# One fixed place order for VectorE's side work in a fused attention, expert and cosine kernel

## The chip, the core and the metric

The kernel runs on one core of a Trainium2 chip. The metric is the device time of one execution in microseconds (us). Three runs of the kernel before gave 2160.01, 2161.22 and 2163.99 us; the median is 2161.22.

## The reference

Three layers follow one another. A delta-rule attention gives 3072 tokens of 384 numbers. A mixture of 8 experts follows, in which every token goes through every expert, and each expert's result is scaled by a probability; the probabilities come from an exponential and eight rounds of row and column normalising. A network with `h * cos(h)` ends it.

```
P = np.exp(logits)                       # 3072 x 8
for _ in range(8):
    P /= P.sum(1, keepdims=True) + 1e-09
    P /= P.sum(0, keepdims=True) + 1e-09
    P *= N / E
for e in range(E):
    h = np.maximum(x @ w1[e], 0.0)       # 384 -> 1024
    ye = h @ w2[e]                       # 1024 -> 384
    out += P[:, e:e + 1] * ye
...
h = x @ w_in; g = h * np.cos(h); return g @ w_out
```

## The kernel before

Everything is float32, computed as a high and a low part that are both rounded to the matmul's input format: one product is three matmuls (high by high, high by low, low by high).

Attention and expert 0 come first, to about 412 us of the profile. Then experts 1 to 7 run in 56 **groups** of one function, `group(n)`. A group holds 256 of an expert's 1024 hidden units. The tokens are handled in two passes of 1536: groups 0 to 27 are the first pass, 28 to 55 the second. Inside a group three token blocks by two halves of hidden units are multiplied with a fast scheme that needs 15 products where the plain one needs 18. Its products have names and a fixed order: N0, N2, N1, N4, N3, CE, b, a, CD, DF, EF, CF, d, c, e, each three matmuls of 512 columns (L1456). They go into five accumulator banks that change roles from group to group (X, Z, A, B, C). ScalarE copies some banks out (`copy`, L1461), VectorE adds and subtracts between them (`vadd`, L1464: seven in a group, called here by their results B, A, sc, s2, C, Z and the second B). A product that adds to a bank, or reuses it, waits for these: **CE** needs B done, since B still reads Z; **a** needs A; **EF** needs sc, since sc reads Z; **c** needs C.

Between the products stand six blocks of nine matmuls of the second layer (L150), after N2, N4, CD, CF, c and e. Twelve such blocks, four for each of three token blocks, are spread over an odd group and the even one behind it. After the fourth block of a token block `gates()` multiplies the three result banks by the expert's probabilities (L1488, VectorE, three instructions) and adds them to the running sum (L1489, GpSimd, three). That falls after N3 and after e in odd groups, and after CF in even ones.

Each engine works through its own instructions in the written order. Beside the above, a group carries **side work**:

- `s_prep(n + 1)` makes the next group's first weights: in the first pass GpSimd forms sums (q0, q1: L1257 to L1265), ScalarE rounds the high parts (`hi`, L1268), VectorE subtracts for the low parts (`lo`, L1271); they are also stored, and the second pass only loads them (`g_load`, L1227).
- `w2h`, `w2l` split the second weights in the same way (L1281 on ScalarE; L1285 on VectorE in the first pass, on GpSimd in the second).
- `bgq` is a list of small pieces that `bg()` takes from: first the token sums of the second pass (`t_prog`), then the **weight conversion** of the last network, nine VectorE instructions per half block (L1419 to L1427, called c0 to c8 below), 288 in all.

`s_prep` gives lists that the group runs at seven places, `go(0)` to `go(6)`; `bg()` stands at eight places.

The probabilities reach the chip's memory once (`pts`). `p_load` (L1309) brings one expert's row for 512 tokens into `pslot[t]`, copied to all partitions: 512 runs of 512 bytes, issued by SyncE. Expert 0's result was stored unscaled; `acc_load` brings it back (L1314) and `acc_mul` scales it by expert 0's probabilities on GpSimd (L1324, nine instructions). In group 0 the three slots get expert 0's rows, in group 1 expert 1's rows go into the same three slots.

Of the kernel before, what the change touches and what calls it, by code (L numbers as in the profile page):

```python
# [38 lines left out]
def kernel(  # L39
# [654 lines left out]
    with tc.manual_schedule():  # L694
# [337 lines left out]
        def t_prog(p, s, rest):  # L1032
# [32 lines left out]
            def emit(nm, i, hi, also=None):  # L1065
                gap(3)

                def run():
                    v.tensor_tensor(out=s[i].bitcast(F32R), in0=s[i], in1=s[hi], op=SUB)
                    keep(nm, hi, 0)  # L1070
                    keep(nm, i)
                    if also and not rest:
                        keep(*also)
                    if not rest:
                        put()
                q.append(lambda: nc.scalar.activation(out=s[hi].bitcast(F32R), in_=s[i], func=ACTF.Copy))
# [164 lines left out]
        def w2_get(n):  # L1241
            nc.sync.dma_start(out=w2reg(n)[:, 768:1536].bitcast(F32), in_=w2c[n % GP])

        def s_prep(n):

# [32 lines left out]

            def w2h():
                x = w2reg(n)  # L1280
                nc.scalar.activation(out=x[:, 0:768], in_=x[:, 768:1536].bitcast(F32), func=ACTF.Copy)  # L1281

            def w2l():
                x = w2reg(n)
                (nc.gpsimd if n >= GP else nc.vector).tensor_tensor(  # L1285
                    out=x[:, 768:1536], in0=x[:, 768:1536].bitcast(F32), in1=x[:, 0:768].bitcast(F32), op=ALU.subtract
                )

            def raw_next():
# [4 lines left out]
            if n >= GP:  # L1294
                return [[lambda: g_load(n)], [], [get], [], [], [w2h], [w2l]]
            return [[q0, q1, hi(s_p, ps)], [lo(s_p, ps), hi(s_v, vs)],
                    [get, hi(s_f, fs), lo(s_f, fs), lo(s_v, vs)],
                    [raw_next, hi(s_u, us)], [lo(s_u, us)], [store, w2h], [w2l]]

# [7 lines left out]

        def p_load(t, e, b):
            nc.sync.dma_start(  # L1309
                out=pslot[t].rearrange("p (t c) -> p t c", t=4), in_=pts[4 * b:4 * b + 4, e, :].partition_broadcast(128)  # L1310
            )

        def acc_load(p, t):
            nc.sync.dma_start(out=acc3[t], in_=ysc[3 * p + t])  # L1314

        def acc_mul(p, t):
            b, z = 3 * p + t, ctile(3) if p else pslot[t]
            if p:
                nc.sync.dma_start(
                    out=z.rearrange("p (t c) -> p t c", t=4), in_=pts[4 * b:4 * b + 4, 0, :].partition_broadcast(128)  # L1320
                )
# [29 lines left out]
        def temit(nm):  # L1351
# [7 lines left out]
                [lambda: temit("CE"), lambda: x2sum(2), lambda: tadd("d", 0)],  # L1359
                sq[3] + [lambda: temit("CD"), lambda: tadd("e", 1)], sq[4], sq[5][:1]]  # L1360
        nb = 0
# [145 lines left out]

        def bg(k=1, opt=False):
            if opt and gnow[0] < GP and len(bgq) <= len(cv):
                return  # L1510
            for _ in range(k if gnow[0] > 1 else 0):
                if bgq:
                    bgq.pop(0)()

        def group(n):
# [9 lines left out]
            if n + 4 < GP:  # L1525
                w2_copy(n + 4)
            nx = s_prep(n + 1) if n + 1 < NGR else [[] for _ in range(7)]
            if n == 0:
                nx[0] = [lambda: tadd("CF", 2), cfirst, lambda: tadd("c", 2), lambda: temit("CF")] + nx[0]
                nx[1] = [lambda: temit("d")] + nx[1] + [lambda: w2_get(0)]  # L1530
                nx[2] = [lambda: temit("c")] + nx[2] + [lambda: temit("e")]
                nx[3] = nx[3] + sq[5][1:]
                nx[4] = nx[4] + sq[6]

# [25 lines left out]
            gates()  # L1560
            bg()
            m(X, "N1")
# [3 lines left out]
            vadd(B, sb, Z, ALU.subtract)  # L1566
            bg(opt=True)
            F()
# [6 lines left out]
            gates()  # L1575
            go(1)
            bg(2 if p else 1)
            m(Z, "CE")
# [3 lines left out]
            relu(n, 0, 0, A)  # L1582
            bg()
            m(X, "CD")
# [235 lines left out]
        bg(999)  # L1820

# [86 lines left out]
```

## Time and profile before

| | |
|---|---|
| time of the profiled execution | 2159.15 us |
| span of its trace | 2157.4 us |
| TensorE matmul busy | 2071.0 us, 96% |
| VectorE busy | 1433.3 us, 66% |
| GpSimd busy | 939.2 us, 44% |
| ScalarE busy | 858.3 us, 40% |

TensorE's busy share covers the whole span; where it idles has to be looked up by stage. The groups run from 412.08 to 1738.84 us. In a row of instructions "ps" is an accumulator bank, "mh" a hidden tile, "w1t" and "w2t" weight tiles, "tp" the buffers of the conversion, "cth" and "scr" scratch tiles, "accp" the running sums. The arrow at a row's end names what ended the idle time before it.

### The profile page before, as it was taken

What the parts mean: (1) busy time and instruction counts of PE and PEld (TensorE: products, weight loads), DVE (VectorE), ACT (ScalarE), POOL (GpSimd) and SP (SyncE); (2) the same over time, 40 slices, a digit from 0 to 9 for tenths busy, and PEclk for the clock granted to TensorE, in tenths of its full rate; (3) what the DMA queues carried; (4) which work ended last, traced back from release to release, by engine and by line L of the source; (5) the groups of instructions that cost most, each with busy time, mean ns of one, the idle gap of its engine ahead of it and who ended that gap; (6) DMA issues with size and microseconds to landing.
All of it is one profiled execution on the core that took longest, in us unless ns stands there. A gap on an engine that the chain in (4) does not pass through costs nothing.

```text
span 2157.4 us, 39716 instructions
## 1 busy us (share of the span) xinstructions
PE 2071.0 (96%) x16147; PEld 1729.1 (80%) x16147; DVE 1433.3 (66%) x2231; ACT 858.3 (40%) x1436; POOL 939.2 (44%) x1029
## 2 busy tenths in 40 slices
PE   7899999879999999999999999999999999999999
PEld 6788888657787887777777888878888889999998
DVE  6665445656766776776767777777777656666665
ACT  3333223333343343333323333323233246666665
POOL 4676560546465564444435333333334343333332
PEclk7899999989999999999999999999999999999999
DMA  5433244755455555344494534344353370001000
GB/s 95 120 91 83 47 114 147 273 169 199 173 178 172 168 182 172 137 154 166 173 332 152 184 127 167 131 137 163 115 176 127 140 290 7 23 30 30 15 16 15
DMA packets 210742, 290.72 MB, mean 135 GB/s; under 512 B 85968, under 2 KB 159152, under 8 KB 210560
## 3 DMA queue, kind: packets, MB, share of 16 engines
q1 hardware_dynamic: 207728, 281.41, 39.5%
q0 software_dynamic: 1664, 6.49, 0.9%
q8 instruction: 126, 2.06, 0.4%
q10 hardware_dynamic: 1168, 0.30, 0.1%
q14 instruction: 56, 0.46, 0.1%
HBM read 187.12 MB, written 112.03 MB: 139 GB/s over the span
## 4 chain that ended last, share of the span: by engine, by line
PE 75%; DVE 9%; POOL 6%; issue 3%; DMA 3%; ACT 1%; SPq 1%; POOLq 0%; DVEq 0%; ACTq 0%
PE ps L150 29%; PE ps L1456 19%; PE ps L1735 9%; PE ps L1693 9%; PE ps L138 4%; DVE cth L1488 2%; POOL accp L1489 2%; DVE mh L157 2%; PE ps L312 1%; DMA w2t<-w2c 1%; DVE scr L1464 1%; DVE tp L1420 1%; POOL w1t L391 1%; POOL w1t L387 1%; PE ps L280 1%
## 5 line engine op out<-in xcount | busy, mean ns | idle before, releaser
L150 PE MATMUL ps<-mh,w2t 128*128 128x512 f32 x3060 | 751.9, 390 | 11.4 <-DVE cth L1488 11.4
L150 PEld LDWEIGHTS ps<-mh,w2t 128*128 128x128 f32 x3060 | 576.5, 189 | 132.9 <-DVE cth L1488 12.3
L1456 PE MATMUL ps<-T,w1t 128*128 128x512 f32 x2520 | 640.5, 393 | 35.5 <-DVE scr L1464 27.8
L1489 POOL TENSOR_TENSOR accp<-accp,cth 128x512 f32<-128x512 f32 x246 | 337.5, 1402 | 633.4 <-DVE cth L1488 633.4
L1456 PEld LDWEIGHTS ps<-T,w1t 128*128 128x128 f32 x2520 | 468.4, 188 | 153.9 <-DVE scr L1464 42.7
L156 ACT ACTIVATE mh<-ps 128x512 fp32r<-128x512 f32 x340 | 201.5, 597 | 525.5 <-DVE ps L1464 194.7
L157 DVE SCALAR_TENSOR_TENSOR mh<-ps,mh 128x512 fp32r<-128x512 f32 x340 | 227.7, 686 | 165.2 <-ACT mh L156 165.1
L1464 DVE TENSOR_TENSOR ps<-scr,ps 128x512 f32<-128x512 f32 x168 | 116.7, 694 | 153.8 <-PE ps L1456 152.1
L1461 ACT ACTIVATE scr<-ps 128x512 f32<-128x512 f32 x224 | 134.1, 599 | 210.3 <-PE ps L1456 202.5
L1702 POOL TENSOR_SCALAR tp<-tp 128x512 f32<-128x512 f32 x92 | 91.2, 992 | 204.4 <-ACT tp L1701 204.4
L1488 DVE TENSOR_TENSOR cth<-ps,scr 128x512 f32<-128x512 f32 x246 | 154.2, 683 | 23.9 <-issue 17.1
L1716 DVE TENSOR_TENSOR tp<-tp,ps 128x512 f32<-128x512 f32 x96 | 66.1, 688 | 133.5 <-ACT tp L1715 133.5
L138 PE MATMUL ps<-xb,w1t 128*128 128x512 f32 x432 | 113.1, 406 | 4.9 <-DVE h L157 3.5
L1464 DVE TENSOR_TENSOR scr<-ps,scr 128x512 f32<-128x512 f32 x112 | 76.8, 686 | 38.1 <-PE ps L1456 37.4
L150 PE MATMUL ps<-h,w2t 128*128 128x512 f32 x396 | 98.4, 393 | 0.0
L138 PEld LDWEIGHTS ps<-xb,w1t 128*128 128x128 f32 x432 | 79.0, 191 | 23.3 <-DVE h L157 3.6
L391 POOL TENSOR_TENSOR w1t<-w1t 128x30 f32<-128x30 f32 (+9 forms) x150 | 81.9, 546 | 11.8
L150 PEld LDWEIGHTS ps<-h,w2t 128*128 128x128 f32 x396 | 73.4, 188 | 15.5
L1693 PE MATMUL ps<-xx,cw 128*128 128x512 f32 x360 | 84.0, 390 | 0.0
L387 POOL TENSOR_TENSOR w1t<-Nsys,w1t 128x30 f32<-128x30 f32 (+9 forms) x150 | 77.2, 515 | 11.4
L1701 ACT ACTIVATE tp<-ps 128x512 f32<-128x512 f32 x96 | 56.2, 586 | 63.7 <-PE ps L1693 63.7
L1735 PE MATMUL ps<-cw,nh 128*128 128x384 f32 x432 | 78.6, 335 | 0.0
(281 smaller groups left out, 2762.4 us busy)
## 6 DMA issues: line engine op xcount, KB each, us to landing
wss<-w1t SPq DMA_DIRECT2D x56, 768.0 KB
w1t<-wss SPq DMA_DIRECT2D x56, 768.0 KB
w2t<-w2c SPq DMA_DIRECT2D x56, 384.0 KB
wsn<-tp SPq DMA_DIRECT2D x64, 192.0 KB
scr<-pts SPq DMA_DIRECT2D x45, 256.0 KB
wraw<-in_moe_w_dram SPq DMA_DIRECT2D x28, 384.0 KB
w2c<-in_moe_w_dram SPq DMA_DIRECT2D x28, 384.0 KB
wss<-w1t SPq DMA_DIRECT2D x28, 384.0 KB
```

The costliest lines, as they stand in the source:

```text
L138: nc.tensor.matmul(out=ps[:, :nn], lhsT=w[:, a, kk, fs], rhs=x[:, b, kk, c0:c0 + nn], start=(i == 0), stop=(i == 3 * KD - 1),)
L150: nc.tensor.matmul(out=banks[kd], lhsT=w[:, a, f % 2, kd * 128:(kd + 1) * 128], rhs=h[:, b, :], start=(first and b == 0 and a == 0), stop= ...
L156: nc.scalar.activation(out=h[:, 0, :nn], in_=ps[:, :nn], func=ACTF.Relu)
L157: nc.vector.scalar_tensor_tensor(out=h[:, 1, :nn], in0=ps[:, :nn], scalar=0.0, in1=h[:, 0, :nn].bitcast(F32), op0=ALU.max, op1=ALU.subtract,)
L391: eng.tensor_tensor(out=xsys[:, j + 1:, 0:j], in0=xsys[:, j + 1:, 0:j], in1=a, op=ALU.add)
L1456: nc.tensor.matmul(out=bank, lhsT=s_of(n, nm, a), rhs=T[:, b, :], start=start and q == 0, stop=q == 2, skip_group_check=True)
L1461: nc.scalar.activation(out=out, in_=in_, func=ACTF.Copy, scale=scale)
L1464: nc.vector.tensor_tensor(out=out, in0=a, in1=b, op=op)
L1488: nc.vector.tensor_tensor(out=c, in0=yb[kd], in1=pslot[t], op=ALU.mult)
L1489: nc.gpsimd.tensor_tensor(out=a[:, kd, :], in0=a[:, kd, :], in1=c, op=ALU.add)
L1693: nc.tensor.matmul(out=hb2(i), lhsT=net_w1(f, a, kk), rhs=x2[b](c, kk), start=(j == 0), stop=(j == 3 * KD - 1))
L1735: nc.tensor.matmul(out=ybk[t][:, :DM], lhsT=h[:, a, ts], rhs=net_w2(f, c), start=(f == 0 and j == 0), stop=(f == FT2 - 1 and j == 2),)
```

## The change

Five things are done.

1. The eight places of `bg()` become four: after the block behind N2, after the sum B (behind N4), behind CD, and at the group's end. How many pieces are taken there depends on what the list holds: 2, 2, 2, 2 of the token sums; 1, 0, 2, 1 of the conversion in the first pass; 3 (4 in odd groups), 2, 3, 2 in the second.
2. `go(1)`, which holds the `lo` of the SP weights in the first pass, moves from behind N3 to before N1; the `hi` of the SV weights moves from `go(1)` to `go(2)`.
3. The second weights are split in the group that uses them: `w2h(n)` before N1, `w2l(n)` behind the sum B, where before group n - 1 did it at its end.
4. Expert 0's row for the first token block goes into a scratch tile (`ctile(3)`), so that `pslot[0]` gets expert 1's row at once. For the other two blocks expert 1's row is loaded right behind the scaling, and GpSimd issues that load.
5. A rounding step of the token sums comes one empty piece later (`gap(4)`).

```diff
-        def bg(k=1, opt=False):
-            if opt and gnow[0] < GP and len(bgq) <= len(cv):
-                return
+        def bg(sums, first, second):
+            k = second if gnow[0] >= GP else sums if len(bgq) > len(cv) else first
...
             gates()
-            bg()
+            if n:
+                w2h(n)
+            go(1)
+            bg(2, 1, 3 + n % 2)
             m(X, "N1")
...
             vadd(B, sb, Z, ALU.subtract)
-            bg(opt=True)
+            if n:
+                w2l(n)
+            bg(2, 0, 2)
...
             gates()
-            go(1)
-            bg(2 if p else 1)
             m(Z, "CE")
...
             relu(n, 0, 0, A)
-            bg()
             m(X, "CD")
...
             go(2)
-            bg()
+            bg(2, 2, 3)
...
         def acc_mul(p, t):
-            b, z = 3 * p + t, ctile(3) if p else pslot[t]
+            b, z = 3 * p + t, ctile(3) if p or not t else pslot[t]
...
+            if not p and t:
+                p_load(t, 1, t, nc.gpsimd)
...
             if not sk:
+                z_load(0, ctile(3))
                 for t in range(3):
-                    p_load(t, 0, t)
+                    p_load(t, 0 if t else 1, t)
```

The order of three places follows; "ps_154" are the accumulator banks, and lines from L1242 on are numbered differently in the two kernels (conversion L1419 to L1427 before, L1423 to L1431 after; `vadd` L1464 and L1468; `gates` L1488 and L1492).

VectorE in an odd group of the second pass (35), from the sum A to the sum sc, before:

```order
L1464 TENSOR_TENSOR ps_154<-scr,ps_154 128x512
L1488 TENSOR_TENSOR cth<-ps_154,scr 128x512 x3
L1419 TENSOR_SCALAR tp<-tp 128x384
L1420 TENSOR_SCALAR tp<-tp 128x384
L157 SCALAR_TENSOR_TENSOR mh<-ps_154,mh 128x512 x2
L1421 SCALAR_TENSOR_TENSOR tp<-tp 128x384
L1464 TENSOR_TENSOR scr<-ps_154,scr 128x512
```

The same place after:

```order
L1468 TENSOR_TENSOR ps_154<-scr,ps_154 128x512
L1492 TENSOR_TENSOR cth<-ps_154,scr 128x512 x3
L157 SCALAR_TENSOR_TENSOR mh<-ps_154,mh 128x512 x2
L1468 TENSOR_TENSOR scr<-ps_154,scr 128x512
L1423 TENSOR_SCALAR tp<-tp 128x384
```

Three conversion pieces have left the stretch between the sums A and sc.

VectorE from the end of odd group 35 into even group 36, before, from `gates()` to the sum A:

```order
L1488 TENSOR_TENSOR cth<-ps_154,scr 128x512 x3
L157 SCALAR_TENSOR_TENSOR mh<-ps_154,mh 128x512
L1425 TENSOR_SCALAR tp<-tp 128x384
L1426 SCALAR_TENSOR_TENSOR tp<-tp 128x384
L1464 TENSOR_TENSOR ps_154<-scr,ps_154 128x512
L1427 SCALAR_TENSOR_TENSOR tp<-tp 128x384
L1464 TENSOR_TENSOR ps_154<-scr,ps_154 128x512
```

The same place after:

```order
L1492 TENSOR_TENSOR cth<-ps_154,scr 128x512 x3
L157 SCALAR_TENSOR_TENSOR mh<-ps_154,mh 128x512
L1426 TENSOR_SCALAR tp<-tp 128x384
L1427 SCALAR_TENSOR_TENSOR tp<-tp 128x384
L1428 TENSOR_SCALAR tp<-tp 128x384
L1429 TENSOR_SCALAR tp<-tp 128x384
L1430 SCALAR_TENSOR_TENSOR tp<-tp 128x384
L1468 TENSOR_TENSOR ps_154<-scr,ps_154 128x512
L1431 SCALAR_TENSOR_TENSOR tp<-tp 128x384
L1423 TENSOR_SCALAR tp<-tp 128x384
L1468 TENSOR_TENSOR ps_154<-scr,ps_154 128x512
```

Five pieces instead of two stand ahead of the sum B, and two instead of one between B and A.

SyncE's transfers at the end of group 0 and in group 1, before ("accp<-ysc" is expert 0's result, "w2c" and "wraw" are weights):

```order
L654 DMA pts<-scr 64x128
L1309 DMA scr<-pts 128x4x128 x3
L1314 DMA accp_6359<-ysc_83 128x1536
L1314 DMA accp_6360<-ysc_84 128x1536
L1314 DMA accp_6361<-ysc_85 128x1536
L1236 DMA w2c_102<-in_moe_w_dram 256x1x384
L1242 DMA w2t<-w2c_99 128x768
L1230 DMA wraw<-in_moe_w_dram 128x3x256
L1309 DMA scr<-pts 128x4x128 x3
```

After:

```order
L654 DMA pts<-scr 64x128
L1316 DMA cth<-pts 128x4x128
L1308 DMA scr<-pts 128x4x128 x3
L1313 DMA accp_6359<-ysc_83 128x1536
L1313 DMA accp_6360<-ysc_84 128x1536
L1313 DMA accp_6361<-ysc_85 128x1536
L1236 DMA w2c_102<-in_moe_w_dram 256x1x384
L1242 DMA w2t<-w2c_99 128x768
L1230 DMA wraw<-in_moe_w_dram 128x3x256
```

A fourth row of probabilities stands ahead of the other loads, and the three later ones have left the queue.

## Rows read from the trace of the kernel before

**Rows 1.** The page's head.
```profile
span 2157.4 us, 39716 instructions
```

**Rows 2.** Busy time by stretch: group 2; 3-27; 28-54; 35; 36. Then clock, DMA share, GB/s.
```profile
465.06:501.95 36.89, 25.53 (x101) 20.04 (x100) 15.32 (x24) 9.46 (x17) 27.88 (x26) 0.81 0.68 243
501.95:1087.50 585.55, 570.77 (x2477) 461.57 (x2476) 412.89 (x614) 226.23 (x406) 301.82 (x300) 1.00 0.50 172
1087.50:1716.03 628.53, 610.99 (x2675) 500.55 (x2674) 454.92 (x716) 198.14 (x325) 233.44 (x163) 1.00 0.46 159
1252.18:1276.11 23.93, 22.75 (x100) 18.51 (x99) 14.85 (x26) 7.33 (x12) 4.81 (x4) 1.00 0.25 91
1276.11:1298.55 22.44, 22.44 (x100) 18.59 (x99) 18.55 (x28) 7.32 (x12) 11.24 (x8) 1.00 0.56 164
```

**Rows 3.** TensorE's waits: for whom, us in total, times, longest.
```profile
PE ps L1456 <- DVE scr L1464: 27.8, 28, 1.7
PE ps L150 <- DVE cth L1488: 11.4, 1, 11.4
```

**Rows 4.** Timeline of groups 35, 36: start, us, engine, instruction, count, [idle before].
```profile
1262.26 0.48 DVE L1419 TENSOR_SCALAR tp<-tp 128x384 f32<-128x384 f32 x1
1262.77 1.34 DVE L1420 TENSOR_SCALAR tp<-tp 128x384 int32<-128x384 int32 x1
1265.23 0.55 DVE L1421 SCALAR_TENSOR_TENSOR tp<-tp 128x384 f32<-128x384 f32 x1
1266.44 1.66 PE L1456 MATMUL ps<-T,w1t 128*128 128x512 f32 x6 [1.18 <-DVE scr L1464]
...
1278.33 1.13 DVE L1425 TENSOR_SCALAR tp<-tp 128x384 int32<-128x384 int32 x1
1279.50 1.52 DVE L1426 SCALAR_TENSOR_TENSOR tp<-tp 128x384 int32<-128x384 int32 x1
1281.75 1.39 DVE L1427 SCALAR_TENSOR_TENSOR tp<-tp 128x384 fp32r<-128x384 int32 x1
1282.91 3.56 PE L1456 MATMUL ps<-T,w1t 128*128 128x512 f32 x15
1284.40 0.36 DVE L1419 TENSOR_SCALAR tp<-tp 128x384 f32<-128x384 f32 x1
```

**Rows 5.** GpSimd beside them, in group 36.
```profile
1276.70 3.91 POOL L1489 TENSOR_TENSOR accp<-accp,cth 128x512 f32<-128x512 f32 x3 [11.43 <-DVE cth L1488]
1280.57 2.15 POOL L1285 TENSOR_TENSOR w2t<-w2t 128x768 fp32r<-128x768 f32 x1
```

**Rows 6.** Timeline of first-pass groups 20 (ScalarE) and 21.
```profile
908.70 0.63 ACT L1268 ACTIVATE w1t<-scr 128x512 fp32r<-128x512 f32 x1 [5.53 <-POOL scr L1265]
...
932.00 0.81 DVE L1271 TENSOR_TENSOR w1t<-wraw,w1t 128x512 fp32r<-128x512 f32 x1
932.74 1.64 DVE L1426 SCALAR_TENSOR_TENSOR tp<-tp 128x384 int32<-128x384 int32 x1
936.70 1.65 PE L1456 MATMUL ps<-T,w1t 128*128 128x512 f32 x6 [1.70 <-DVE scr L1464]
```

**Rows 7.** Timeline around group 2's wait, all engines.
```profile
474.31 0.84 ACT L1281 ACTIVATE w2t<-w2t 128x768 fp32r<-128x768 f32 x1 [11.12 <-DMA w2t<-w2c]
475.54 0.62 ACT L1268 ACTIVATE w1t<-wraw 128x512 fp32r<-128x512 f32 x1
468.79 11.07 POOL L1324 TENSOR_TENSOR accp<-accp,scr 128x512 f32<-128x512 f32 x9 [18.42 <-DMA accp<-ysc]
488.69 0.45 POOL L1265 TENSOR_TENSOR scr<-wraw 128x128 f32<-128x128 f32 x1
477.94 4.21 PE L150 MATMUL ps<-mh,w2t 128*128 128x512 f32 x9 [11.36 <-DVE cth L1488]
481.94 2.01 PE L1456 MATMUL ps<-T,w1t 128*128 128x512 f32 x6
```

**Rows 8.** A stretch of 4 us there, in the columns of rows 2.
```profile
460.00:464.00 4.00, 4.00 (x20) 3.30 (x19) 1.82 (x4) 1.45 (x3) 0.00 (x0) 1.00 0.78 68
```

More of the change, by code (lines that the diff above doesn't have):

```diff
@@ L1065, in emit @@
             def emit(nm, i, hi, also=None):
-                gap(3)
+                gap(4)
                 def run():
@@ L1242, in w2_get, with w2h, w2l @@
             nc.sync.dma_start(out=w2reg(n)[:, 768:1536].bitcast(F32), in_=w2c[n % GP])
+        def w2h(n):
+            x = w2reg(n)
+            nc.scalar.activation(out=x[:, 0:768], in_=x[:, 768:1536].bitcast(F32), func=ACTF.Copy)
+        def w2l(n):
+            x = w2reg(n)
+            (nc.gpsimd if n >= GP else nc.vector).tensor_tensor(
+                out=x[:, 768:1536], in0=x[:, 768:1536].bitcast(F32), in1=x[:, 0:768].bitcast(F32), op=ALU.subtract
+            )
         def s_prep(n):
@@ L1277, in store @@
                     nc.sync.dma_start(out=wss[n % GP][:, o:o + t.shape[1]], in_=t.bitcast(F32))
[L1279 to L1287, printed above, removed]
             def raw_next():
@@ L1294, in s_prep @@
             if n >= GP:
[L1295 to L1298, printed above, removed]
+                return [[lambda: g_load(n)], [], [get], [], [], []]
+            return [[q0, q1, hi(s_p, ps)], [lo(s_p, ps)], [get, hi(s_v, vs), hi(s_f, fs), lo(s_f, fs), lo(s_v, vs)],
+                    [raw_next, hi(s_u, us)], [lo(s_u, us)], [store]]
         def t_load(p, nm):
@@ L1306, in t_load, with p_load @@
             nc.sync.dma_start(out=TT[nm].bitcast(F32), in_=src)
-        def p_load(t, e, b):
-            nc.sync.dma_start(
+        def p_load(t, e, b, eng=nc.sync):
+            eng.dma_start(
                 out=pslot[t].rearrange("p (t c) -> p t c", t=4), in_=pts[4 * b:4 * b + 4, e, :].partition_broadcast(128)
@@ L1314, in acc_load, with z_load @@
             nc.sync.dma_start(out=acc3[t], in_=ysc[3 * p + t])
+        def z_load(b, z):
+            nc.sync.dma_start(
+                out=z.rearrange("p (t c) -> p t c", t=4), in_=pts[4 * b:4 * b + 4, 0, :].partition_broadcast(128)
+            )
         def acc_mul(p, t):
-            b, z = 3 * p + t, ctile(3) if p else pslot[t]
+            b, z = 3 * p + t, ctile(3) if p or not t else pslot[t]
             if p:
-                nc.sync.dma_start(
-                    out=z.rearrange("p (t c) -> p t c", t=4), in_=pts[4 * b:4 * b + 4, 0, :].partition_broadcast(128)
-                )
+                z_load(b, z)
             for kd in range(KD):
@@ L1359 @@
                 [lambda: temit("CE"), lambda: x2sum(2), lambda: tadd("d", 0)],
-                sq[3] + [lambda: temit("CD"), lambda: tadd("e", 1)], sq[4], sq[5][:1]]
+                sq[3] + [lambda: temit("CD"), lambda: tadd("e", 1)], sq[4], sq[5]]
         nb = 0
@@ L1526, in group @@
                 w2_copy(n + 4)
-            nx = s_prep(n + 1) if n + 1 < NGR else [[] for _ in range(7)]
+            nx = s_prep(n + 1) if n + 1 < NGR else [[] for _ in range(6)]
             if n == 0:
@@ L1531, in group @@
                 nx[2] = [lambda: temit("c")] + nx[2] + [lambda: temit("e")]
-                nx[3] = nx[3] + sq[5][1:]
-                nx[4] = nx[4] + sq[6]
+                nx[4] = nx[4] + [lambda: w2h(0)]
+                nx[5] = nx[5] + [lambda: w2l(0)]
             def go(i):
@@ L1613, in group @@
             go(3)
-            bg(opt=True)
             if n == NGR - 1:
@@ L1624, in group @@
                 some()
-            if n == 1:
-                for t in range(3):
-                    p_load(t, 1, t)
             gates()
             go(4)
-            bg(opt=True)
             m(Z, "e")
@@ L1637, in group @@
             relu(n, 1, 1, Z)
-            bg(opt=True)
-            go(6)
+            bg(2, 1, 2)
         accb, x2, wx = {}, {}, {}
@@ L1819 @@
                     acc_load(0, t)
-        bg(999)
+        while bgq:
+            bgq.pop(0)()
         def wtile(tag):
```

## The prediction

> **What bounds the kernel now.** I read the table of TensorE's waits first, then busy time by stretch, then the timeline where a wait ends.
>
> TensorE sets the time of the groups. Group 36 takes 22.44 us and TensorE is busy in all of it [rows 2]; its 99 matmuls then take 0.227 us each, 0.68 for a product of three and 2.04 for a block of nine. I call 22.44 the floor. Over it lie: group 2 with 36.89 - 22.44 = 14.4 us; groups 3 to 27 with 585.55 - 25 x 22.44 = 24.5; groups 28 to 54 with 628.53 - 27 x 22.44 = 22.7 [rows 2]. So at most 61.6 us can be had, and nothing that shortens VectorE counts unless one of these waits goes. The waits have two names: 27.8 us in 28 pieces for VectorE's `scr` (the sum sc, for which EF waits) and one of 11.4 us for `gates()` in group 2 [rows 3]. Most of the rest over the floor are shorter gaps and the slow clock after that one wait.
>
> **Groups 3 to 27, first pass.** Group 21 shows the odd kind: between A and sc VectorE runs a weight's low part (0.81) and two pieces, of which one shown takes 1.64, and EF comes 1.70 late [rows 6]. All three leave that stretch, and 0.81 + 1.64 alone is more than 1.70. Group 20 shows the even kind: ScalarE waits 5.53 us for GpSimd's last sum before it can round the SV weights, and the hidden tiles queue behind that [rows 6]. The rounding now stands behind CD, where GpSimd has had 10 us of the group. What is late next: ahead of the sum B now stand piece, low part, piece, and the second-weight split of about 1 us comes between B and A. In an even group VectorE is free of the last hidden tile 2.3 us into the group; with each of the three waiting for one GpSimd instruction B is done at about 6.7, and CE is due at 7.5; split and A end at 8.7, and a is due at 8.8. Tight but inside. I leave 0.3 us a group for it, 7.5 in all: 24.5 - 7.5 = **17 us gained**, between 10 and 22.
>
> **Groups 28 to 54, second pass.** Odd groups: three pieces go (0.48, 1.34, 0.55), EF was 1.18 late, and the group takes 23.93 against 22.44 [rows 2, 4]. Without them sc is done 2.4 us earlier, 0.8 before EF is due. Twelve groups (31 to 53) x 1.49 = 17.9 us go.
>
> Even groups are where the cost comes up. Their floor time hid their pieces; now five stand ahead of the sum B instead of two. In group 36 GpSimd adds the gated results from 1276.70 to 1280.61 and splits the second weights from 1280.57 to 1282.72 [rows 5]. Two pieces beside that took 1.13 and 1.52 and a third, against the split, 1.39 until 1283.14, where a piece alone takes 0.36 or 0.55 [rows 4]. So a piece waits for the GpSimd instruction under way, and then GpSimd has its turn. Counted from the group's start at 1276.11: the first two pieces end at 3.35 and 4.91 as before. The third now meets the split, and ends at 7.0 (as the 1.39 row did at 1283.14). Two more, alone, of 0.36 to 0.55 bring 7.9; B of 0.69 ends at 8.6. CE is due at 1282.91 + 0.68, that is 7.48 [rows 4]. It comes 1.2 late, and A behind two more pieces makes a late by another 0.1 or 0.2: 1.3 us. Eleven even groups (30 to 50; the list is used up in 51, since it now gives 10 or 11 pieces a group instead of 9) x 1.3 = 14.3 us come. In odd groups the split on GpSimd runs alone at 3 to 5 us, six pieces end at 5.8, B at 6.5: no wait.
>
> The Trainium skill has a rule here (SBUF — State Buffer, Who interferes with whom): VectorE and GpSimd share a port pair, and whichever issues first holds it for the whole instruction. The trace agrees on the whole instruction (the 1.39 beside the split of 2.15), and so the page speaks against this place for the pieces. By its "first" the third piece could also go ahead of the split; that is the first rival.
>
> Groups 28 to 31 gain one late EF (1.5) and pay 0.8 for four early pieces in 28 and some 1 more for scaling on GpSimd in 30. I take 0. The rest of the 22.7 stays. Sum of the pass: 17.9 - 14.3 = **3.6 gained**, between 22 (no late CE) and -5 (2.1 us a group).
>
> **Group 2.** Before, `gates()` waited for expert 1's row, which waited for the scaling, which began at 468.79 when expert 0's results had landed [rows 7]. That wait goes: the row now comes in group 0. What is late next: SyncE's queue. ScalarE waited until 474.31 for the second weights and rounded the next `wraw` at 475.54 [rows 7]; both loads stand behind the rows of probabilities and the three results. A row is 256 KB, and in 460 to 464 the transfers ran at 68 GB/s [rows 8]: 3.8 us each. There are now four instead of three ahead, so results, second weights and `wraw` land 3.8 later. `wraw` at about 479.1, its rounding, and the copy of X put N1 at about 480.3; before, N1 started at 481.94 [rows 7]. TensorE idles from 469 to 480 instead of 466.6 to 477.9. The mean granted clock of group 2 is 0.81 [rows 2], of two levels, 1.2 and 2.4 GHz; the nine matmuls after the wait took 4.21 instead of 2.2 us [rows 7]. I take the same cost of 2.5 us after a wait of the same length. GpSimd's chain moves too: scaling from 472.6 for 11.07, three sums of gated results, and the weight sums, which ended at 489.14 [rows 7], now end near 494. The SV rounding and the copy behind it make C late by 0.5, and `gates()` behind them holds back the block after c by 1.5. So this stretch is **2 us lost**, between 9 gained (the fourth row costs nothing) and 6 lost. The two loads that GpSimd issues are shown nowhere; the `gates()` that need them are 10 us later.
>
> By the Trainium skill (DMA: Bandwidth & Descriptors, Specifications) transfers run at line rate from 512 bytes a piece on. The runs here are 512 bytes and ran at 68 GB/s [rows 8]. By the page's limit of 358 GB/s a row would take an estimated 0.7 us, and group 2 would gain about 1 instead of losing 2. I go by the row.
>
> **Nothing** is counted for group 0 (the same work in another order), for the later rounding step (an empty place), and for the end.
>
> **Sum.** 17 + 3.6 - 2 = 18.6 us, on the profiled 2159.15 (span 2157.4 [rows 1]): 2140.5. The median of the runs is 2 us above the profile, so a median would be about 2142. I say **2141**.
>
> **Rivals.**
>
> *No late CE in even groups* (first rival). The third piece gets in before the split, or the split starts after the pieces. For it: it needs only 0.3 us of luck. Against: twice in rows 4 and 5 GpSimd had its turn between two pieces. Then 14.3 us more: 2127.
>
> *A new wait at a in the first pass.* The split between B and A waits behind longer GpSimd instructions, as the piece of 1.64 did [rows 6]; A then ends about 1.1 after a is due in the 12 even groups. For it: the margin above is 0.1 us. Against: the weight sums on GpSimd are short (0.45 shown, rows 7). 13 us dearer: 2154.
>
> *Slower: the five early pieces decide.* If each of the five waits 1.64 as in rows 6, since pieces lengthen GpSimd's instructions in turn, B ends at 2.3 + 8.2 + 0.7 = 11.2, CE is 3.7 late and a 0.7 more: 4.4 instead of 1.3, over 11 groups 34 us, so 2175. From 3 us a group on the change is no gain. Against: GpSimd has nothing more to do from 6.6 us on [rows 5].
>
> **Chances.** Forecast 0.50 (its own range 2133 to 2150); first rival 0.18; new wait at a 0.22; slower 0.10. A measurement of this kernel tells 0.2% (4.3 us) from no change, so faster is under 2156.9. The forecast and the first rival are faster, of the wait at a half (0.10) is faster and 0.12 within; so 0.78, 0.12, 0.10. The range 2122 to 2158 takes in the first rival with a little of group 2's upper bound and the wait at a; it leaves out the slower case and the far ends.
>
> **What would show it.** After: EF's wait for `scr` nearly gone from TensorE's table, the SV rounding's wait for GpSimd as well. A new row "PE ps <- DVE ps" of about 11 x 1.2 us in groups 30 to 50, and even groups of 23.7 us beside odd ones of 22.44; groups 52 to 54 at the floor. In group 2 no wait for `cth`, but one of about 11 us that ScalarE's copy ends. The prediction is wrong if even groups stay at 22.44, if first-pass groups do not come under 22.9 on the mean, or if group 2 is shorter than 33 us.

## The result and the profile after

The changed kernel takes 2138.64 us (median of four executions: 2135.80, 2138.34, 2138.95 and 3559.67) where the kernel before took 2162.34 on the same chip. The ratio is 0.9887, with a 95% interval of 0.9867 to 0.9906. The execution of 3559.67 was disturbed, and the ratio leaves it out. The forecast was 2141. The profiled execution took 2138.95 us. By the profiles 20.2 us went (2159.15 to 2138.95), where the sum had 18.6. So the time is right, and partly by luck: the three terms behind it came out 1.7 to 2.9 us better each, 6.4 in all, and 4.6 us that the sum put at nothing were lost ahead of group 2.

I read the same views as before, first busy time by stretch: group 2, groups 3 to 27, groups 28 to 54, group 35, group 36 (PE, PEld, DVE, ACT, POOL, then clock, DMA share, GB/s).

```profile
469.69:506.75 37.06, 26.93 (x100) 20.71 (x99) 16.98 (x24) 9.06 (x16) 28.82 (x28) 0.82 0.69 234
506.75:1072.38 565.63, 563.54 (x2477) 463.82 (x2475) 420.30 (x608) 228.16 (x407) 297.85 (x300) 1.00 0.51 176
1072.38:1695.61 623.23, 610.83 (x2674) 500.21 (x2673) 474.27 (x725) 197.23 (x324) 224.46 (x162) 1.00 0.47 163
1237.51:1259.94 22.43, 22.43 (x100) 18.59 (x99) 17.17 (x28) 7.31 (x12) 5.91 (x4) 1.00 0.28 98
1259.94:1283.50 23.56, 22.83 (x101) 18.44 (x99) 19.06 (x29) 7.32 (x12) 9.84 (x7) 1.00 0.48 156
```

Against [rows 2] the first pass gives 585.55 - 565.63 = 19.9 us and the second 628.53 - 623.23 = 5.3; group 2 gives nothing (36.89, now 37.06). VectorE is busier than before in both passes, which costs nothing. Groups 35 and 36 have changed sides: the odd one is now at the floor of 22.44 us, the even one 1.1 over it. Group 0 begins 3.4 us later (415.5, before 412.1). TensorE is already 3.2 us behind at its 2000th matmul (100.5, before 97.4), far ahead of anything that the change touches. In the profiles of all kernels in this document group 0 begins between 412.1 and 420.2, so I give that to the execution and not to the change. Groups 0 and 1 take another 1.2 us.

TensorE's waits in the groups (for whom, us in total, times, longest):

```profile
PE ps L1460 <- DVE ps L1468: 17.6, 18, 2.2
PE ps L1460 <- ACT ct L1465: 7.8, 1, 7.8
PE ps L150 <- DVE cth L1492: 1.2, 2, 0.8
```

ScalarE's wait at the SV rounding for GpSimd's last weight sum, before and after:

```profile
ACT w1t L1268 <- POOL scr L1265: 93.5, 27, 5.7
ACT w1t L1278 <- POOL scr L1275: 7.6, 4, 3.8
```

EF's wait for `scr`, 27.8 us in 28 pieces [rows 3], is gone, as is the wait of 11.4 for `gates()`. In their places stand waits for a sum in an accumulator bank (B ahead of CE, mostly) and one for ScalarE's copy ahead of N1 in group 2. Both were forecast by name. The rounding's wait for GpSimd, the one behind the even groups of the first pass [rows 6], is nearly gone too.

**Even groups of the second pass.** The timeline of group 36, TensorE, VectorE and GpSimd:

```profile
1260.53 3.92 POOL L1493 TENSOR_TENSOR accp<-accp,cth 128x512 f32<-128x512 f32 x3 [10.18 <-DVE cth L1492]
1262.16 1.15 DVE L1426 TENSOR_SCALAR tp<-tp 128x384 int32<-128x384 int32 x1
1263.34 1.53 DVE L1427 SCALAR_TENSOR_TENSOR tp<-tp 128x384 int32<-128x384 int32 x1
1264.42 2.16 POOL L1250 TENSOR_TENSOR w2t<-w2t 128x768 fp32r<-128x768 f32 x1
1264.91 1.88 DVE L1428 TENSOR_SCALAR tp<-tp 128x384 int32<-128x384 int32 x1
1266.72 0.34 DVE L1429 TENSOR_SCALAR tp<-tp 128x384 int32<-128x384 int32 x1
1267.10 0.56 DVE L1430 SCALAR_TENSOR_TENSOR tp<-tp 128x384 int32<-128x384 int32 x1
1267.57 0.69 DVE L1468 TENSOR_TENSOR ps<-scr,ps 128x512 f32<-128x512 f32 x1
1268.31 3.11 PE L1460 MATMUL ps<-T,w1t 128*128 128x512 f32 x12 [0.73 <-DVE ps L1468]
1269.03 0.69 DVE L1468 TENSOR_TENSOR ps<-scr,ps 128x512 f32<-128x512 f32 x1
```

The first two pieces meet the adds, the third ends 0.2 after the split on GpSimd (1.88 us, where the same form takes 0.36 alone), and the last two are short. B ends 8.3 us into the group. CE starts at 8.37, 0.89 after its place at 7.48; the row's idle time of 0.73 is shorter, because a row's length takes in some 0.16 us in which the next matmul could start (nine take 2.20 us where 9 x 0.227 is 2.04). The forecast was 8.6 and 1.2. The twelve matmuls behind the wait take 3.11 us, 0.23 more than twelve would without one: CE's own three 0.12, and CD 0.09. The sum A, the last row, ends at 9.78, and a starts at 9.86, late by 0.01 beyond CE's delay, though two pieces stand between B and A. In all 1.1 to 1.2 a group.

**Group 2**, ScalarE, GpSimd, VectorE and TensorE:

```profile
473.18 3.70 POOL L1326 TENSOR_TENSOR accp<-accp,cth 128x512 f32<-128x512 f32 x3 [18.73 <-DMA accp<-ysc]
479.85 0.63 ACT L1278 ACTIVATE w1t<-wraw 128x512 fp32r<-128x512 f32 x1 [9.36 <-DMA wraw<-in_moe_w_dram]
480.38 0.58 ACT L1465 ACTIVATE ct<-ps 128x512 f32<-128x512 f32 x1
481.01 2.93 PE L1460 MATMUL ps<-T,w1t 128*128 128x512 f32 x6 [7.76 <-ACT ct L1465]
494.33 0.46 POOL L1275 TENSOR_TENSOR scr<-wraw 128x128 f32<-128x128 f32 x1
494.82 0.64 ACT L1278 ACTIVATE w1t<-scr 128x512 fp32r<-128x512 f32 x1 [3.84 <-POOL scr L1275]
496.12 1.77 DVE L1281 TENSOR_TENSOR w1t<-scr,w1t 128x512 fp32r<-128x512 f32 x1
498.41 0.68 DVE L1468 TENSOR_TENSOR ps<-scr,ps 128x512 f32<-128x512 f32 x1
499.14 1.39 PE L1460 MATMUL ps<-T,w1t 128*128 128x512 f32 x3 [1.98 <-DVE ps L1468]
500.93 3.24 PE L150 MATMUL ps<-mh,w2t 128*128 128x512 f32 x9 [0.39 <-DVE cth L1492]
```

This answers to [rows 7]. The row of expert 1 is there in time, but ScalarE gets `wraw` only at 479.85, rounds it ahead of the copy of X, and N1 waits. Fourteen us on, the SV rounding waits for GpSimd's last sum. Behind it VectorE makes the SV weights' low part (1.77 us, the first of the two VectorE rows) ahead of the sums s2 and C (the second row), and c and the block behind it are late. Six matmuls after the wait take 2.93 us, against 1.52 elsewhere: the granted clock is 0.82 over the group.

### The profile page after: what moved, and what is told of

It is laid out like the page before. It is cut to its first block, busy times and chain, and to the rows that moved or that the text cites. A ratio compares the mean times of both kernels' runs of the same rounds, so it can differ in the third digit from the quotient of the medians.

```text
span 2137.2 us, 39712 instructions
## 1 busy us (share of the span) xinstructions
PE 2071.1 (97%) x16147; PEld 1735.5 (81%) x16147; DVE 1461.4 (68%) x2231; ACT 859.2 (40%) x1436; POOL 929.0 (43%) x1031
## 3 DMA queue, kind: packets, MB, share of 16 engines
q8 instruction: 126, 2.06, 0.4%
## 4 chain that ended last, share of the span: by engine, by line
PE 85%; DVE 7%; POOL 2%; issue 2%; DMA 1%; SPq 1%; ACT 1%; POOLq 0%; DVEq 0%; ACTq 0%
PE ps L150 32%; PE ps L1460 23%; PE ps L1734 9%; PE ps L1692 9%; PE ps L138 4%; PE ps L312 1%; PE ps L280 1%; DVE cth L1492 1%; DVE ps L1468 1%; PE ps L497 1%; PE ps L525 1%; POOL accp L1493 1%; PE ps L474 1%; PE ps L462 1%; DVE mh L157 1%
## 5 line engine op out<-in xcount | busy, mean ns | idle before, releaser
L1493 POOL TENSOR_TENSOR accp<-accp,cth 128x512 f32<-128x512 f32 x246 | 318.4, 1324 | 568.9 <-DVE cth L1492 568.8
L1468 DVE TENSOR_TENSOR ps<-scr,ps 128x512 f32<-128x512 f32 x168 | 116.1, 691 | 73.0 <-PE ps L1460 70.0
L1492 DVE TENSOR_TENSOR cth<-ps,scr 128x512 f32<-128x512 f32 x246 | 154.1, 681 | 15.3 <-PE ps L150 14.3
L1281 DVE TENSOR_TENSOR w1t<-wraw,w1t 128x512 fp32r<-128x512 f32 (+2 forms) x84 | 81.6, 973 | 23.9 <-ACT w1t L1278 23.6
L1468 DVE TENSOR_TENSOR scr<-ps,scr 128x512 f32<-128x512 f32 x112 | 76.8, 686 | 29.0 <-PE ps L1460 28.3
L391 POOL TENSOR_TENSOR w1t<-w1t 128x30 f32<-128x30 f32 (+9 forms) x150 | 82.7, 551 | 11.8
L387 POOL TENSOR_TENSOR w1t<-Nsys,w1t 128x30 f32<-128x30 f32 (+9 forms) x150 | 76.5, 510 | 11.4
```

What stands on the lines that cost most here:

```text
L1468: nc.vector.tensor_tensor(out=out, in0=a, in1=b, op=op)
L1492: nc.vector.tensor_tensor(out=c, in0=yb[kd], in1=pslot[t], op=ALU.mult)
L1493: nc.gpsimd.tensor_tensor(out=a[:, kd, :], in0=a[:, kd, :], in1=c, op=ALU.add)
```

## The experiments

All times are medians of three rounds (five for the last kernel) and ratios are to the kernel before on the same chip, where it took 2165 to 2168 us. Which stretch moved is read in each run's own trace.

**1. The scaling alone**, added to the kernel before.

```diff
-            b, z = 3 * p + t, ctile(3) if p else pslot[t]
+            b, z = 3 * p + t, ctile(3) if p or not t else pslot[t]
...
+            if not p and t:
+                p_load(t, 1, t, nc.gpsimd)
...
-            if n == 1:
-                for t in range(3):
-                    p_load(t, 1, t)
...
+                z_load(0, ctile(3))
                 for t in range(3):
-                    p_load(t, 0, t)
+                    p_load(t, 0 if t else 1, t)
```

> The kernel before, with one part of the change: four rows of probabilities instead of three stand ahead of group 2 (expert 0's row of block 0 in a spare tile, expert 1's at once in its slot), and expert 1's other two rows are loaded by GpSimd after its scaling. Nothing else is moved. My theory: the wait of 11.36 us at gates() in group 2 goes, but wraw and the second weights come when they did, so TensorE waits 8 to 11 us for ScalarE's copy before N1 instead, and C and the block behind it are late by 1 to 3 us because the scaling still fills GpSimd; group 2 takes 36 to 38 us (36.89 in the kernel before, 37.06 in the changed one) and the time is 2158 to 2166. Rival: the removed wait was the price, group 2 falls to 26 to 29 us, and the time is about 2151. Second rival, as the prediction had it: the fourth row delays all loads behind it by 3.8 us, group 2 takes 38 to 41.

Measured: 2168.50 us, ratio 1.0018 (1.0009 to 1.0028): a little slower. Group 2 takes 41.1 us. TensorE and ScalarE there:

```profile
480.04 2.92 PE L1461 MATMUL ps<-T,w1t 128*128 128x512 f32 x6 [8.81 <-ACT ct L1466]
494.08 0.63 ACT L1268 ACTIVATE w1t<-scr 128x512 fp32r<-128x512 f32 x1 [11.76 <-POOL scr L1265]
496.22 4.21 PE L1461 MATMUL ps<-T,w1t 128*128 128x512 f32 x9 [5.27 <-ACT scr L1466]
```

The wait at N1 is as my theory had it, but the second one is 5.27 and stands at DF, so the theory missed 3 us. The second rival has the right figure for the wrong reason: ScalarE starts on `wraw` 23.4 us after the first row was issued, where it was 22.4 before, so the loads are 1 us later and not 3.8. What is late is the SV rounding: still at its old step, it waits 11.8 us for GpSimd's sums, and CD's and DF's copies queue behind it.

**2. The rounding alone**, in the kernel before.

```diff
-            return [[q0, q1, hi(s_p, ps)], [lo(s_p, ps), hi(s_v, vs)],
-                    [get, hi(s_f, fs), lo(s_f, fs), lo(s_v, vs)],
+            return [[q0, q1, hi(s_p, ps)], [lo(s_p, ps)],
+                    [get, hi(s_v, vs), hi(s_f, fs), lo(s_f, fs), lo(s_v, vs)],
```

> The kernel before, with one part of the change: the rounding of the SV weights stands one step later in the list (behind CD, with those of the SF weights) in the groups of the first pass. VectorE's pieces stay where they are. My theory: in even groups of the first pass ScalarE waits up to 5.5 us for GpSimd's last weight sum at this rounding, and the copies behind it make DF and EF late (0.2 to 1.4 us); these waits go, even groups from 4 to 26 fall from 23.5 to about 22.6 on the mean, odd groups stay at 23 to 24.4 with their wait at EF of 1.3 to 1.7 from 17 on, groups 3 to 27 fall from 585.6 to 574 to 579, and the time is 2150 to 2156. Rival: the pieces and the weight's low part on VectorE set the even groups too; groups 3 to 27 stay at 583 to 587 and the time within 3 us of before. Second rival: this step alone carries the whole gain of the first pass, odd groups too: 566, time 2142.

Measured: 2151.89 us, ratio 0.9940 (0.9924 to 0.9957). Groups 3 to 27:

```profile
505.27:1079.45 574.18, 564.98 (x2476) 463.12 (x2475) 416.39 (x615) 227.90 (x406) 303.09 (x301) 1.00 0.50 175
```

11.4 us less than before, all in even groups (mean 22.49, before 23.48), while odd groups stay at 23.48 (before 23.43). One moved instruction in ScalarE's queue carries more than half of the first pass's gain; the other 8.5 come with the rest of the change, 11.3 gained in odd groups less some 3.2 lost in even ones, in groups 4 and 16. Whether the odd groups gain by the moved low part or by the moved pieces, no run separates.

**3. Both together**, the edits of 1 and 2.

> The kernel before with two parts of the change: expert 0's scaling freed (as in the run of that part alone) and the SV rounding one step later. In the run of the scaling alone group 2 took 41.1 us: 8.8 at N1 and 5.3 at DF, where ScalarE's copy stood behind the SV rounding and that behind GpSimd's last sum. My theory: with the rounding later that copy no longer waits, the 5.3 shrink to 1 to 2.5 at c or the block behind it, group 2 takes 36 to 38.5; groups 3 to 27 take 573 to 576 as with the rounding alone; time 2148 to 2155. Rival: the 5.3 come back whole at c or in the next block, group 2 stays at 40 to 42, and the time is 2156 to 2159.

Measured: 2152.50 us, ratio 0.9933 (0.9919 to 0.9948); group 2 takes 38.9 us, just above what I expected. TensorE's two longest waits at its products there:

```profile
478.73 2.93 PE L1461 MATMUL ps<-T,w1t 128*128 128x512 f32 x6 [8.66 <-ACT ct L1466]
497.12 0.96 PE L1461 MATMUL ps<-T,w1t 128*128 128x512 f32 x3 [1.99 <-DVE ps L1469]
```

DF's 5.27 are gone and c has 1.99 for them. So freeing the scaling loses 3 to 4 us without the later rounding and gains nothing with it: this time and that of the rounding alone agree within their intervals.

**4. The rounding put back into step 1** of the changed kernel.

```diff
-            return [[q0, q1, hi(s_p, ps)], [lo(s_p, ps)], [get, hi(s_v, vs), hi(s_f, fs), lo(s_f, fs), lo(s_v, vs)],
+            return [[q0, q1, hi(s_p, ps)], [lo(s_p, ps), hi(s_v, vs)], [get, hi(s_f, fs), lo(s_f, fs), lo(s_v, vs)],
```

> The changed kernel with the rounding of the SV weights put back one step earlier, where the kernel before has it; all else as changed. It is the other half of the run with the rounding alone, which took 11.4 us off groups 3 to 27, all in even groups (23.48 to 22.49 us on the mean; odd groups stayed at 23.48). My theory: in the first pass the two parts are separate. The rounding owns the even groups, the four set stretches own the odd ones. With the rounding back, even groups 4 to 26 return to 23.2 to 23.6 with waits that end with ScalarE's copy at DF or VectorE's sum at EF, odd groups stay at 22.5 to 22.7, groups 3 to 27 take 574 to 579; group 2 gets a wait at DF of 4 to 6 us and takes 39 to 42; time about 2150 to 2156. Rival: with VectorE's pieces out of the stretch before EF the early rounding does no harm; even groups stay at 22.8 or less, groups 3 to 27 at 566 to 569, and the time within 4 us of the changed kernel's 2139.

Measured: 2236.19 us, ratio 1.0323 (1.0301 to 1.0345). Both theories fell, because I had read the step's number and not its place: the change had moved step 1 from behind N3 to ahead of N1. TensorE's wait and group 20's ScalarE:

```profile
PE ps L1460 <- ACT scr L1465: 71.2, 20, 9.4
```

```profile
970.84 0.63 ACT L1278 ACTIVATE w1t<-scr 128x512 fp32r<-128x512 f32 x1 [6.44 <-POOL scr L1275]
971.38 0.58 ACT L1465 ACTIVATE scr<-ps 128x512 f32<-128x512 f32 x1
972.01 4.39 PE L1460 MATMUL ps<-T,w1t 128*128 128x512 f32 x11 [3.67 <-ACT scr L1465]
```

ScalarE waits 6.44 us at the rounding, the copy of X (behind N1) stands behind it, and N3, which adds to X, waits for that. The moved step and the later rounding are one edit: without the second the first costs some 95 us, 85 of them in groups 3 to 27.

**5. The rounding at its true old place**, behind A and ahead of CE, in the changed kernel (the list gets a seventh step).

```diff
-[get, hi(s_v, vs), hi(s_f, fs), lo(s_f, fs), lo(s_v, vs)],
+[get, *([] if n else [hi(s_v, vs)]), hi(s_f, fs), lo(s_f, fs), lo(s_v, vs)],
...
-[store]]
+[store], [hi(s_v, vs)] if n else []]
...
             gates()
+            go(6)
             m(Z, "CE")
```

> The run with the rounding put back into step 1 did not restore the place of the kernel before, because the change had moved step 1 itself, from behind N3 to ahead of N1. Here the SV rounding stands where the kernel before had it, behind A and gates() and ahead of CE; all else as changed. My theory, now with the right place: ScalarE then waits at this rounding until GpSimd's last sum, later than the copies of N1 to N3 but ahead of CD's, and CD's and DF's copies are late in even groups as in the kernel before: even groups 4 to 26 at 23.2 to 23.8 us, odd ones at 22.5 to 22.7, groups 3 to 27 at 573 to 579, group 2 at 39 to 42, time 2148 to 2155. Rival: with the low part and the pieces out of VectorE's way there is slack for the late copies, even groups stay at 22.8 or less and the time within 4 us of the changed kernel's 2139.

Measured: 2158.06 us, ratio 0.9968 (0.9954 to 0.9981). Groups 3 to 27 take 579.5 us; even groups return to 23.79 (23.18 without groups 4 and 16, which took 25.7 and 28.0), odd ones stay at 22.63; group 2 takes 40.7 with this wait back:

```profile
499.41 4.21 PE L1460 MATMUL ps<-T,w1t 128*128 128x512 f32 x9 [4.68 <-ACT scr L1465]
```

My theory, by its parts; the time is 3 above its range. With run 2 it splits the first pass from both sides: the rounding owns the even groups, the rest of the change the odd ones.

**6. The old eight places** for the second pass's pieces in the changed kernel.

```diff
-            bg(2, 1, 3 + n % 2)
+            bg(2, 1, 1)
...
-            bg(2, 0, 2)
+            bg(2, 0, 1)
...
+            bg(0, 0, 2)
...
+            bg(0, 0, 1)
...
-            bg(2, 2, 3)
+            bg(2, 2, 1)
...
+            bg(0, 0, 1)
...
+            bg(0, 0, 1)
...
-            bg(2, 1, 2)
+            bg(2, 1, 1)
```

> The changed kernel, with the conversion pieces of the second pass put back at the eight places of the kernel before (1,1,2,1,1,1,1,1). The first pass has no such pieces from group 3 on and stays as changed. My theory: the gain of the second pass (628.5 to 623.2 us for groups 28 to 54) is the sum of EF no longer late in odd groups (-1.5 each) and CE late in even groups (+1.15 each), both set by the places alone. With the old places odd groups return to about 23.9 with a wait for scr at EF, even groups to 22.44, groups 28 to 54 to 626 to 630, and the time is 2142 to 2146; groups 3 to 27 stay at 565 to 567. Rival: the late CE of even groups comes from the split of the second weights now being in the group it is used in; then even groups stay near 23.6 while odd ones return to 23.9, groups 28 to 54 take 636 to 642, and the time is 2152 to 2158.

Measured: 2146.17 us, ratio 0.9923 (0.9901 to 0.9945).

```profile
PE ps L1460 <- DVE scr L1468: 18.2, 13, 3.4
```

Odd groups 33 to 53 return to 23.91 with a wait of 1.16 at EF, even groups 32 to 50 to 22.44. So the places set both, and the split in its own group costs nothing by itself. Groups 28 to 54 took 635.8 in the profile and not 626 to 630: groups 29 and 31 took 28.6 and 27.7, with waits at EF of 2.06 and 3.37 and, in 29, one of 1.66 at N0 for a weight load. That execution was the longest of six (2157; another took 2155); the median is 0.2 above the theory's range, and what slowed these two groups I leave open.

**7. The split later** in even groups of the second pass, in the changed kernel.

```diff
-            if n:
+            late_split = n >= GP and n % 2 == 0
+            if n and not late_split:
                 w2h(n)
...
-            if n:
+            if n and not late_split:
                 w2l(n)
...
+            if late_split:
+                w2h(n)
+                w2l(n)
             go(3)
```

> The changed kernel, with only the split of the second weights moved in the even groups of the second pass: from behind gates() ahead of the early pieces to a place behind EF, ahead of the third stretch. My theory, as in the prediction: the third early piece stands behind GpSimd's split (2.15 us in the kernel before), which is what makes the sum B and with it CE late by 0.72 to 0.85 in groups 32 to 50. With the split gone from there the five pieces end about 1.5 us earlier, CE's wait goes, even groups take 22.44, groups 28 to 54 take 609 to 614 and the time is 2125 to 2130. Rival: five pieces beside GpSimd's adds of gated results (3.9 us) are too many whatever the split does; the wait at CE stays at 0.5 to 0.9 and the time at 2136 to 2139. Second rival: the split only moves its cost, into the sum sc or C of the even groups; then a new wait of 0.5 or more at CF, d or c.

Measured: 2130.34 us, ratio 0.9839 (0.9825 to 0.9854). VectorE in group 36, and TensorE's CE:

```profile
1264.37 1.14 DVE L1426 TENSOR_SCALAR tp<-tp 128x384 int32<-128x384 int32 x1
1265.54 1.53 DVE L1427 SCALAR_TENSOR_TENSOR tp<-tp 128x384 int32<-128x384 int32 x1
1267.11 0.36 DVE L1428 TENSOR_SCALAR tp<-tp 128x384 int32<-128x384 int32 x1
1267.38 0.35 DVE L1429 TENSOR_SCALAR tp<-tp 128x384 int32<-128x384 int32 x1
1268.25 0.69 DVE L1468 TENSOR_TENSOR ps<-scr,ps 128x512 f32<-128x512 f32 x1
1268.95 3.34 PE L1460 MATMUL ps<-T,w1t 128*128 128x512 f32 x14
```

The third piece takes 0.36 where it took 1.88, B ends 6.8 us into the group and CE waits for nothing. Even groups take 22.57 on the mean; groups 29 to 31, in which GpSimd also scales, still pay. This shows the step of the prediction that the even groups rested on. Groups 28 to 54 take 614.7 us and the time is 0.3 above the upper edge of what I expected.

**8. The pieces moved instead**, the split left where the change put it. A group also takes nine pieces here, where the changed kernel takes ten or eleven.

```diff
-            bg(2, 1, 3 + n % 2)
+            bg(2, 1, 4 if n % 2 else 0)
...
-            bg(2, 2, 3)
+            bg(2, 2, 3 if n % 2 else 5)
...
-            bg(2, 1, 2)
+            bg(2, 1, 0 if n % 2 else 2)
```

> The changed kernel, with the pieces of the second pass at other places: odd groups 4, 2, 3 and 0 at the four stretches (changed kernel 4, 2, 3, 2), even groups 0, 2, 5 and 2 (changed kernel 3, 2, 3, 2). The split of the second weights stays where the change put it. The run with the late split took the wait at CE away by moving the split; this one leaves the split and takes the pieces away. My theory: VectorE's pieces and GpSimd's split in the same stretch are what makes CE late, and either may go. Without pieces ahead of B the wait at CE goes in the even groups from 32 on; the five in the third stretch, where GpSimd is idle, take 0.36 to 0.55 each and end in time. Even groups then take 22.44 to 22.6 as with the late split (22.57), and the time is 2126 to 2136. Rival: five pieces in the third stretch make the sum C or the sum B of CF late; a new wait of 0.5 or more at CF, d or c in even groups, and 2138 or more.

Measured: 2128.29 us, ratio 0.9821 (0.9806 to 0.9835). Even groups 32 to 50 take 22.45 and groups 28 to 54 608.2 us, 2.3 over the floor. In group 36 the five pieces behind CD take 0.35 to 0.56 each; GpSimd has no instruction there. Either partner of the collision may go, as my theory had it.

**9. A fifth row** in front of the results, in the changed kernel; nothing reads it.

```diff
                 z_load(0, ctile(3))
+                z_load(1, tpt[:, 0, 1024:1536])
```

> The changed kernel with one more row of probabilities (256 KB) loaded ahead of the three results, into a tile that nothing reads at that time; no value of the output changes. The prediction priced a row at 3.8 us of queue; the four rows of the changed kernel took 12.2 us, as the three of the kernel before did. By the prediction's price, or by 12.2 / 4 = 3.05, group 2's wait for ScalarE's copy grows from 7.8 (8.3 in two other executions) to 11 or 12, group 2 takes 40 to 43 us and the time is 2141 to 2145. By the other view (the rows end when the stores before them let them, and a further one costs nothing) the wait stays at 7.5 to 8.5, group 2 at 37 to 39.5, and the time is 2136 to 2141.

Measured: 2144.82 us, ratio 0.9901 (0.9884 to 0.9917). Group 2 takes 41.6 us:

```profile
481.01 0.63 ACT L1278 ACTIVATE w1t<-wraw 128x512 fp32r<-128x512 f32 x1 [13.25 <-DMA wraw<-in_moe_w_dram]
482.18 2.92 PE L1460 MATMUL ps<-T,w1t 128*128 128x512 f32 x6 [11.66 <-ACT ct L1465]
```

N1 waits 11.66, against 7.76 to 8.38 in the four profiles with four rows: the fifth costs 3.3 to 3.9 us. The prediction's price holds for it, and yet the fourth cost next to nothing. From the first row's issue to the last of its packets two rows took 9.3 us (kernel 10), three 13.3 and 13.7, four 13.7 to 14.5, five 17.5. Stretches of 4 us from 456 to 468 in this kernel:

```profile
456.00:460.00 4.00, 4.00 (x20) 3.30 (x19) 2.74 (x6) 0.83 (x3) 0.00 (x0) 1.00 0.57 66
460.00:464.00 4.00, 4.00 (x19) 3.31 (x18) 2.28 (x4) 1.82 (x3) 0.00 (x0) 1.00 0.75 133
464.00:468.00 4.00, 4.00 (x19) 3.33 (x18) 2.85 (x5) 1.20 (x2) 0.00 (x0) 1.00 0.51 79
```

The rate is 66 in one stretch and twice that in the next. That reads as one row at a time and then two side by side, with the fourth row travelling beside another; it is a reading of the rates, and no run shows which rows pair, or why.

**10. A faster kernel.** The late split of 7; in groups 28 to 31 fewer pieces (0, 1, 1, 2); and group 2 rebuilt, so that two rows and one result go ahead of the next weights, and GpSimd scales one block instead of three ahead of the weight sums.

```diff
-            b, z = 3 * p + t, ctile(3) if p or not t else pslot[t]
+            b, z = 3 * p + t, ctile(3) if p or not t else tpv[:, 3 + t, :]
...
             if n == 1:
                 acc_mul(0, 0)
-                acc_mul(0, 1)
...
-            if n == 1:
-                acc_mul(0, 2)
+            if n == 2:
+                acc_mul(0, 1)
...
             go(3)
+            if n == 1:
+                for t in range(1, 3):
+                    acc_load(0, t)
+                    z_load(t, tpv[:, 3 + t, :])
+                    p_load(t, 1, t)
...
             go(4)
+            if n == 2:
+                acc_mul(0, 2)
...
-            for _ in range(k if gnow[0] > 1 else 0):
+            for _ in range(k if gnow[0] > 2 else 0):
```

> An attempt at a faster kernel, on the late split. Group 2: only two rows and one result are loaded ahead of the next group's weights, the other two results and four rows behind them; expert 0's rows of blocks 1 and 2 have spare tiles of their own, so expert 1's wait for nothing; the scaling of block 1 is done in group 2 and that of block 2 at its end; side pieces begin in group 3. Groups 28 to 31: 0, 1, 1 and 2 pieces instead of 3 or 4, 2, 3 and 2. My theory: the wait at N1 goes from 8.3 to under 2 us and C is no longer late, since GpSimd scales one block instead of three ahead of the sums; group 2 takes 25 to 31 us instead of 39.5; groups 28 to 31 take 1 to 3 us over the floor instead of 7.5; time 2111 to 2122. Rival: GpSimd's work in group 2 (sums 4.6, scaling 11.3, adds 11.7 us) is over the floor of 22.4 wherever it is put, gates() wait for it later on, groups 2 and 3 together gain under 4 us and the time is 2122 to 2128.

Measured: 2108.32 us, ratio 0.9731 (0.9716 to 0.9746), under the range I gave. Group 2, groups 3 to 27, and 28 to 54:

```profile
471.01:495.17 24.16, 23.33 (x100) 18.25 (x99) 17.75 (x24) 8.95 (x16) 21.86 (x21) 1.00 0.71 236
495.17:1059.63 564.46, 563.54 (x2477) 463.70 (x2476) 421.92 (x605) 228.23 (x407) 307.77 (x305) 1.00 0.52 179
1059.63:1666.68 607.05, 606.99 (x2674) 501.31 (x2673) 454.97 (x729) 195.71 (x324) 221.43 (x162) 1.00 0.48 167
```

TensorE is busy in 606.99 of 607.05 us. In group 2 `wraw` comes in time, N1 waits for nothing, and the slow clock goes with the wait:

```profile
473.09 0.63 ACT L1278 ACTIVATE w1t<-wraw 128x512 fp32r<-128x512 f32 x1 [1.28 <-DMA wraw<-in_moe_w_dram]
474.42 1.53 PE L1458 MATMUL ps<-T,w1t 128*128 128x512 f32 x6
```

The rival, that GpSimd's work would be late wherever it is put, is refuted. Which edit of the rebuilt group 2 carries how much of its 13 us no run separates. Groups 3 to 54 together are 4.6 us over 52 x 22.44, so little more is left in their waits.

## Why the prediction was right

**The first pass, 17 forecast, 19.9 measured.** The two mechanisms were the ones named: ScalarE's wait for GpSimd in even groups [rows 6] and the low part and pieces ahead of sc in odd ones, the first shown alone by run 2, the second by run 5, though there the low part and the pieces are not told apart. Mis-sized was the 0.3 us a group that I left for a tight a. Seventeen of the 25 groups stand at 22.44 and six more under 22.8; a is late once, with a wait of 0.96, in group 4. So the rival of a new wait at a was a real place with almost no price. Two groups (4 and 16) hold 3.3 us of what is left.

**The second pass, 3.6 forecast, 5.3 measured.** Odd groups gained 1.5 each, as forecast. Even groups 32 to 50 lost 1.17 each against 1.3. B came a little earlier than I had worked out (CE starts 0.89 to 1.01 late, not 1.2), and A makes a late by 0.02 at most, not 0.1 to 0.2; the rest is CE's and CD's matmuls. Two figures of the forecast do not follow from its own terms: 8.6 less 7.48 is 1.1 and not 1.2, and without a late CE the pass gains 17.9 and not 22. Runs 7 and 8 show that the split beside the third piece is the cause, and that the first rival (no late CE) was open by one more move.

The Trainium skill (SBUF — State Buffer, Who interferes with whom) says of a VectorE instruction in a two-port mode that whichever of VectorE and GpSimd issues first holds the port pair for the whole instruction. The runs agree on the whole instruction: the piece is 1.88 beside the split, ending 0.2 after it, and 0.36 without it. Which mode the piece runs in no run shows.

**Group 2, 2 lost forecast, 0.2 lost in the profile.** Over four profiles with the changed group 2 (37.06, 39.41, 39.48, 37.03) against two with the scaling as before (36.89, and 36.64 in run 2) it is 1.5. The mechanism is right, two terms of it are not, and that they offset each other is luck. The fourth row, priced at 3.8, cost 0.4 to 1.0: ScalarE reaches `wraw` 23.4 us after the first row's issue in run 1, against 22.4 before, and 23.3 in run 3, against 22.9 in run 2. So N1 waits 7.8 to 8.4 and not 11. The failed step is "A row is 256 KB, and in 460 to 464 the transfers ran at 68 GB/s": 68 GB/s was not the rate of four rows, which took 13.7 to 14.5 us in all and not 4 x 3.8, and the reading under run 9 is that a row beside another is nearly free. Against that c came 1.7 to 2.0 late and not 0.5. GpSimd's sums ended 25.1 us into the group, earlier than forecast (28.9); but behind the rounding I counted only the copy, and VectorE's low part of the SV weights, 1.77 us there and 0.68 in group 20 of the same kernel, also stands ahead of C.

**Nothing elsewhere**: group 0 began 3.4 us later and took 34.6 us against 33.7. Groups 28 to 31 took 95.4 together against 95.9, where I had set gain against loss; in group 30 CE waits 2.21 and the group takes 26.1, before 23.0.

## What to carry to other kernels

When two engines slow each other, a place in the order is a place beside an instruction of the other engine: the same five pieces cost a group 1.2 us or nothing, by whether GpSimd's split stands beside them, and either may be moved. A rounding that waits for another engine belongs as late as its consumer allows, since the in-order queue behind it pays, and a step's number is no place once the step has moved. And a wait that goes is worth only the distance to the next one that ends in the same stretch: taken alone, the wait of 11 us was worth less than nothing.

## What the runs showed of the hardware

- Rows of probabilities in 512-byte runs: two took 9.3 us, three 13.3 to 13.7, four 13.7 to 14.5, five 17.5; stretches of 4 us inside ran at 63 to 133 GB/s.
- A wait of 7.8 us lowered the clock: six matmuls took 2.93 us after it and 1.53 where the wait was gone; the mean granted clock of group 2 was 0.82 with it and 1.00 without (levels 1.2 and 2.4 GHz).
- A load that GpSimd issues holds GpSimd for 0.8 us and lands 8.2 us (median of two) after its issue, in group 2 of the changed kernel.
